# One 512-column product for two of 256 in an attention kernel's split score tiles, nine transposed loads instead of ten, and a new written-out order

## The chip, the cores and the metric

One Trainium2 chip, one of its cores. The metric is the device time of one execution in microseconds (us). The kernel before takes 271.66 us (median of three runs, 271.43 to 271.73).

## What is computed

The reference has two stages, cut here to what matters:

```python
# q, k, v: 4 x 5056 x 256, fp32
qn = q / (norm(q, axis=1) + 1e-6);  kn = k / (norm(k, axis=1) + 1e-6)   # norms down the 5056 rows
a  = softmax(kn.transpose(0, 2, 1) @ qn / tau)                          # 256 x 256 for each batch
x  = (v @ a).reshape(20224, 256)
logits = x @ phi                                                        # 32 slots
slots  = softmax(logits, axis=0).T @ x                                  # over all 20224 rows
out_s  = relu(slots @ w1[e]) @ w2[e]                                    # 8 experts, 4 slots each
out    = softmax(logits, axis=1) @ out_s                                # 20224 x 256
```

The softmax down the rows needs every row of v before the first expert can start, and every row of the output needs the experts. So all of q, k, v and the experts' weights are read before most of the 21 MB of output can be written.

## The kernel before, in words

Four batches follow each other. Each has ten pairs of q and k blocks (`u` = 0 to 39, 512 rows of each, 1 MB a load) and five v blocks (`p` = 0 to 19, 1 MB each).

- **Scores.** For each 128-row tile `j` of a block, TensorE adds k'q into a PSUM tile `S`, 256 x 256, kept as two channel halves `m` of 128 rows by 256 columns in one bank (`sums`, `score`). A tile with `j >= NS[u]` is multiplied in fp32 (`raw`). The other 117 tiles are split in two parts, high (cast by ScalarE in `cast`) and low (raw minus high, by GpSimd in `low`), both fp32r, and three products are added with k's parts as the weights: high x high, high x low, low x high, each of 256 columns.
- **Norms.** ScalarE squares a block (`square`), VectorE adds the squares into two PSUM banks `A` (`add`).
- **Per batch** (`att_*`): ScalarE copies both halves of `S` to SBUF (`att_evict`), VectorE scales them by the norms, ScalarE takes the softmax, and `a` is folded with phi into a small matrix `M`.
- **v blocks.** The logits need v transposed. For the blocks in `LT` the transposed copy `x` is loaded from HBM as well (`load_vt`, 1 MB). For the others TensorE turns the block in 16 transposes (`turn`), and four copies of 128 x 512 by ScalarE or VectorE bring it from PSUM (`turned`, `DVE_TURNED`). `logits` fills `L`, `gather` sums v by weight into `G`.
- **Experts.** 16 loads of 1 MB (`w1`, `w2`), products `H` and `O`. `O` for output half 0 needs the four loads w2_0_*, half 1 the four w2_1_*.
- **Output.** `out_mul` into `op`, copies by ScalarE and VectorE (`out_evict`), stores of 1 MB (`store`). Stores named oh hold one half of the channels and can start when half 0 is done; those named o need both halves.

All DMAs, loads and stores, are issued by SyncE (SP) in one queue. The order of the whole program is written by hand as a list of numbers, `ORDER`: each names an entry of the plan that `at(...)` collects, and the entries are issued in that order, so the list alone sets what stands before what on each engine. SBUF is 23 slots of 8 KB a partition; `SLOTS` says which tile takes which slot and `BANKS` which of PSUM's eight banks. A load waits until the readers of its slot's last tile are done, and every later DMA waits behind it.

Of the kernel before, what the change touches and what calls it, by code (L numbers as in the profile page):

```python
# [24 lines left out]
NT = [3 if u % (2 * UB) == 2 * UB - 1 else 4 for u in range(NU)]  # L25
NS = [0, 2, 2, 2, 2, 2, 2, 2, 2, 2, 3, 3, 3, 3, 3, 3, 3, 3, 3, 3, 3, 3, 3, 3, 3, 3, 3, 3, 3, 3, 4, 4, 4, 4, 4, 4, 4, 4, 4, 3]

LT = {4, 5, 6, 7, 8, 9, 10, 11, 12, 13}
# [1071 lines left out]
```

## Time and profile before

| | before |
|---|---|
| device time, median of 3 runs | 271.66 us (271.43 to 271.73) |
| profiled execution, span from first to last instruction | 269.6 us |
| device time of the profiled execution itself | not listed apart; the median less the span is 2.0 us |
| TensorE, VectorE, ScalarE, GpSimd busy | 91, 75, 77, 63% of the span |
| HBM read and written | 89.43 MB and 20.97 MB |
| mean rate of the DMA queue | 409 GB/s over the span |

The page cuts the span into 40 slices with a digit for the busy tenths of each engine, and lists the costliest groups of instructions, the chain of work that ended last and the DMA queues. The answers of the trace read one stretch more closely: a table of stretches (`windows`), the chain in order of time, and the timeline of one engine.

### The profile page before, as it was taken

Reading aid. Unit: us, or ns where it says so; the run is one execution under the profiler, and the core shown is the slowest. Engines: PE = TensorE matmul, PEld = TensorE weight load, DVE = VectorE, ACT = ScalarE, POOL = GpSimd, SP = SyncE. Lnnn points to the kernel's source line nnn. Section 1 sums busy time; section 2 is a strip of 40 time slices with the busy share of each in tenths; the row PEclk is TensorE's granted clock in tenths of the full one; section 3 lists DMA queues with packets and bytes.
Section 4 is the critical chain, followed back from the end, with each engine's and each line's share of the span. In section 5 each row is a group of like instructions: output and inputs, shape, how many; then the busy total and the mean of one; then the engine's idle time right before and its main releaser. Section 6 shows DMA issues by size and latency. Waiting matters only on the chain.

```text
span 269.6 us, 6368 instructions
## 1 busy us (share of the span) xinstructions
PE 244.9 (91%) x2490; PEld 205.4 (76%) x2490; DVE 201.0 (75%) x406; ACT 207.1 (77%) x331; POOL 169.6 (63%) x135
## 2 busy tenths in 40 slices
PE   6999999999999999999999999999999889989300
PEld 6799899999998987879879968985647677666200
DVE  1388688978799989889998788897785747795400
ACT  3999899999999999999999987586826536566200
POOL 1399989999999998989999999731206030000000
PEclk9999999999999999999999999999999999999555
DMA  7999999999999999999999999999999999999995
GB/s 272 428 424 419 417 419 420 423 418 416 424 414 419 422 417 422 423 414 416 421 421 418 420 427 413 420 420 422 413 423 422 412 418 395 420 424 422 424 425 227
DMA packets 15725, 110.80 MB, mean 411 GB/s; under 512 B 1872, under 2 KB 1872, under 8 KB 3024
## 3 DMA queue, kind: packets, MB, share of 16 engines
q1 hardware_dynamic: 15696, 110.40, 98.8%
q8 instruction: 19, 0.31, 0.5%
q14 instruction: 10, 0.08, 0.1%
HBM read 89.43 MB, written 20.97 MB: 409 GB/s over the span
## 4 chain that ended last, share of the span: by engine, by line
PE 78%; DMA 11%; DVE 2%; ACT 1%; issue 1%; SPq 0%; ACTq 0%
PE S L345 42%; PE L L512 7%; PE G L612 7%; PE T L492 6%; DMA w<-in_moe_w_dram 6%; PE op_None L845 4%; DMA out_dram<-o 3%; PE op L830 3%; DMA raw<-in_qk_dram 3%; PE H L762 2%; PE O L795 1%; PE Mp L445 1%; ACT o L862 1%; PE S L354 1%; PE nn L373 1%; PE aTp L433 1%
## 5 line engine op out<-in xcount | busy, mean ns | idle before, releaser
L292 POOL TENSOR_TENSOR hl<-raw,hl 128x512 fp32r<-128x512 f32 x117 | 146.5, 1291 | 14.3 <-ACT hl L288 14.3
L321 DVE TENSOR_TENSOR A<-sq,A 128x512 f32<-128x512 f32 (+1 forms) x144 | 94.5, 690 | 20.6 <-ACT sq L303 18.5
L345 PE MATMUL S<-hl 128*128 128x256 f32 x702 | 100.0, 292 | 0.0
L345 PEld LDWEIGHTS S<-hl 128*128 128x128 f32 x702 | 89.1, 190 | 3.5 <-issue 2.3
L303 ACT ACTIVATE sq<-raw 128x2048 f32<-128x2048 f32 (+2 forms) x40 | 71.6, 1806 | 0.2 <-DMA raw<-in_qk_dram 0.2
L288 ACT CAST hl<-raw 128x1024 fp32r<-128x1024 f32 (+1 forms) x69 | 61.0, 916 | 2.9 <-DMA raw<-in_qk_dram 1.4
L345 PE MATMUL S<-raw 128*128 128x256 f32 x156 | 38.3, 381 | 1.7 <-DMA raw<-in_qk_dram 1.7
L345 PEld LDWEIGHTS S<-raw 128*128 128x128 f32 x156 | 27.7, 190 | 5.2 <-DMA raw<-in_qk_dram 2.5
L492 PE MATMUL T<-ident,v 128*128 128x128 f32 x156 | 21.8, 274 | 0.5 <-DVE maxs L539 0.5
L710 POOL TENSOR_TENSOR nat<-nat,cm 128x1280 f32<-128x1280 f32 x4 | 9.4, 2352 | 19.0 <-DVE cm L707 19.0
L725 POOL TENSOR_TENSOR nat<-nat,cs 128x1280 f32<-128x1280 f32 x4 | 9.4, 2348 | 16.9 <-DVE cs L722 16.9
L862 ACT COPY o<-op_None 128x512 f32<-128x512 f32 x22 | 12.0, 592 | 10.2 <-PE op_None L845 9.0
L512 PE MATMUL L<-x,M 128*32 128x256 f32 (+1 forms) x320 | 19.3, 379 | 0.0
L492 PEld LDWEIGHTS T<-ident,v 128*128 128x128 f32 x156 | 17.8, 141 | 1.8 <-DVE maxs L539 0.7
L612 PE MATMUL G<-v,dn 128*32 128x256 f32 x312 | 18.7, 380 | 0.0
L830 PE MATMUL op<-cT,so 32*128 32x256 f32 x144 | 17.5, 417 | 0.7 <-ACT so L817 0.4
L862 DVE COPY oh<-op 128x256 f32<-128x256 f32 x36 | 12.9, 411 | 5.3 <-PE op L830 5.0
L862 DVE COPY o<-op_None 128x512 f32<-128x512 f32 x22 | 13.9, 680 | 2.7 <-PE op_None L845 2.6
L830 PEld LDWEIGHTS op<-cT,so 32*128 32x128 f32 x144 | 12.3, 183 | 4.3 <-ACT o L862 1.5
L612 PEld LDWEIGHTS G<-v,dn 128*32 128x32 f32 x312 | 10.7, 110 | 6.3 <-issue 0.5
L512 PEld LDWEIGHTS L<-x,M 128*32 128x32 f32 x320 | 10.3, 110 | 5.7 <-issue 0.7
L862 ACT COPY oh<-op 128x256 f32<-128x256 f32 x36 | 11.9, 384 | 2.7 <-PE op L830 2.7
(122 smaller groups left out, 279.8 us busy)
## 6 DMA issues: line engine op xcount, KB each, us to landing
raw<-in_qk_dram SPq DMA_DIRECT2D x38, 1024.0 KB, 13.6
v<-in_v_dram SPq DMA_DIRECT2D x16, 1024.0 KB, 13.8
w<-in_moe_w_dram SPq DMA_DIRECT2D x16, 1024.0 KB, 19.8
out_dram<-o SPq DMA_DIRECT2D x11, 1024.0 KB, 10.2
x<-in_vt_dram SPq DMA_DIRECT2D x10, 1024.0 KB, 13.5
out_dram<-oh SPq DMA_DIRECT2D x8, 1024.0 KB, 8.8
v<-in_v_dram SPq DMA_DIRECT2D x4, 896.0 KB, 13.8
raw<-in_qk_dram SPq DMA_DIRECT2D x2, 768.0 KB, 11.5
```

Of the source, the lines that this page charges most:

```text
L288: act.copy(parts(u, lo, hi)[:, :, 0::2, :], raws[u][:, lo:hi])
L292: pool.tensor_tensor(hl[:, :, 1::2, :], raws[u][:, lo:hi], hl[:, :, 0::2, :].bitcast(F32), op=ALU.subtract)
L303: act.activation(sqs[u][:, n : NT[u]], raws[u][:, n : NT[u]], AF.Square)
L321: dve.tensor_tensor(a[r], s[r, j], a[r], op=ALU.add)
L345: pe.matmul(S_[:, m], l, r, start=first, stop=False, skip_group_check=True)
L492: pe.transpose(tp[:, P * jj : P * jj + P], vtile(p, 4 * h + jj)[:, P * m : P * m + P], ident)
L512: pe.matmul(L[S * g : S * g + S, :n, :], M[:, m, :], x[:, :n, S * g : S * g + S], start=m == 0 and g not in void, stop=m == 1, skip_group_ ...
L612: pe.matmul(gp[S * g : S * g + S, :C], dn[:, x, j, :], vtile(p, j), start=x == 0 and j < G, stop=x == n - 1 and j >= G,)
L710: pool.tensor_tensor(nat[b], nat[b], st[b]["cm"].broadcast_to([P, 8 * PB, S]), op=ALU.subtract)
L830: pe.matmul(ops[b, p, hf, g], so[r, hf], cT[b][r, 8 * p : 8 * p + 8, :].rearrange("s j t -> s (j t)"), start=True, stop=True,)
L845: pe.matmul(ops[b, p, hf, g][:, h, :], cT[b][r, 4 * i : 4 * i + 4, :].rearrange("s j t -> s (j t)"), rhs[r], start=True, stop=True,)
L862: (dve.tensor_copy if g % 2 else act.copy)(dst, ops[b, p, hf, g])
```

## The change

Five things change.

1. **Joined products.** `S` takes two PSUM banks per batch, one for each channel half `m`. High x high and high x low have the same weights, so they become one product of 512 columns: columns 0 to 255 get high x high, columns 256 to 511 high x low. Low x high is added to columns 0 to 255. 702 products become 468.
2. **Sum of the halves.** `att_evict` is now a VectorE sum of the bank's two column halves (512 elements in, 256 out), in place of ScalarE's copy of 256.
3. **One more v block turned.** `LT` loses block 13: one 1 MB load less, 16 transposes and four copies more (two on VectorE, two on ScalarE).
4. **Memory.** Nine of the 23 slots stay slots of a pool, the other fourteen are slices of one SBUF tile, `arena`. All 1 MB inputs lie in one HBM tensor `one`, rows 8,704 bytes apart as before. The output tensor holds two stores side by side, so its rows lie 16 KB apart instead of 8 KB. Block q0 comes in four loads of 256 KB.
5. **Order, slots and banks** are new.

```diff
-LT = {4, 5, 6, 7, 8, 9, 10, 11, 12, 13}
+LT = {4, 5, 6, 7, 8, 9, 10, 11, 12}
...
+NT_SLOTS, NA_SLOTS = 9, 14
...
 ORDER = [
-    0, 1, 2, 3, 6, 8, 23, 24, 27, 25, 31, 33, 30, 28, 32, 26, 9, 7, 49, 51, 56, 57, 54, 35, 55, 59, 58, 34,
...
+    901, 10, 9, 0, 11, 1, 903, 34, 33, 12, 42, 17, 20, 35, 900, 902, 30, 21, 22, 899, 897, 898, 2, 15, 26,
...
+    arena = const.tile([P, NA_SLOTS, W], F32, name="arena")
+    def block(name):
+        if name not in blocks:
+            k = SLOTS[name]
+            if k < NT_SLOTS:
+                blocks[name] = large.tile([P, W], F32, tag=f"s{k}", name=name)
+            else:
+                blocks[name] = arena[:, k - NT_SLOTS]
+        return blocks[name]
+    def load(g):
+        n = sum(cols(x) for x in GROUPS[g])
+        src = (one, two)[len(GROUPS[g]) - 1][PLACE[g]]
+        sp.dma_start(run_of(GROUPS[g])[:, :n], src[:, :n])
+    def load_first(j):
+        x = slice(2 * C * j, 2 * C * j + 2 * C)
+        sp.dma_start(block("q0")[:, x], one[PLACE[0]][:, x])
...
-            st[b]["S"] = bank(f"S{b}").rearrange("p (m c) -> p m c", m=2)
+            st[b]["S"] = [bank(f"S{b}_{x}") for x in range(2)]
...
             if j >= NS[u]:
-                parts_ = [(raws[u][:, j, 1, cols], raws[u][:, j, 0, :])]
-            else:
-                k, x = split[u, j]
-                hl = hls[k][:, x]
-                parts_ = [(hl[:, w, cols], hl[:, y, :]) for w, y in ((2, 0), (2, 1), (3, 0))]
-            for l, r in parts_:
-                pe.matmul(S_[:, m], l, r, start=first, stop=False, skip_group_check=True)
-                first = False
+                mul(m, raw(u)[:, j, 1, cols], raw(u)[:, j, 0, :], 0, C)
+                continue
+            k, x = split[u, j]
+            hl = hls[k][:, x]
+            mul(m, hl[:, 2, cols], hl[:, 0:2, :].rearrange("p y c -> p (y c)"), 0, 2 * C)
+            mul(m, hl[:, 3, cols], hl[:, 0, :], 0, C)
...
     def att_evict(b, m):
-        act.copy(st[b]["ssb"][:, m], st[b]["S"][:, m])
+        both = st[b]["S"][m].rearrange("p (y c) -> p c y", y=2)
+        dve.tensor_reduce(mine(b, "ssb", [P, 2, C], "ssb")[:, m], both, axis=AX.X, op=ALU.add)
...
+    def store(g):
+        n = W // 2 if OUTS[g][0] in HALF else W * len(OUTS[g])
+        k, x = OPLACE[g]
+        sp.dma_start(oa[k][:, x * W : x * W + n], run_of(OUTS[g])[:, :n])
```

Each group in `GROUPS` and `OUTS` has one name, so every load and store stays one block of 1 MB or less.

**Where the order moves things.** TensorE late in batch 3's scores, before: the split tiles of block pairs (hl47, hl48, ...) stand between the turns of v blocks 14 and 19.

```order
L492 MATMUL T19_1_1_1909<-ident_72,v19_1670 128x128 x3
L492 MATMUL T19_1_1_1909<-ident_72,vh_78 128x128
L492 MATMUL T14_0_1_1914<-ident_72,v14_1637 128x128 x4
L345 MATMUL S3_1401<-hl47_1833 128x256 x6
L345 MATMUL S3_1401<-hl48_1863 128x256 x6
L345 MATMUL S3_1401<-hl41_1828 128x256 x6
```

The same place now (the v block that T13 reads is in the arena, which has one name):

```order
L546 MATMUL T14_0_1_1632<-ident_73,arena_72 128x128 x4
L546 MATMUL T13_1_0_1637<-ident_73,arena_72 128x128 x4
L408 MATMUL S3_0_1282<-hl47_1599 128x512
L408 MATMUL S3_0_1282<-hl47_1599 128x256
L408 MATMUL S3_1_1283<-hl47_1599 128x512
L408 MATMUL S3_1_1283<-hl47_1599 128x256
```

A split tile's six products of 256 columns are now four, two of 512 and two of 256, and turns of block 13 stand among them.

SP at the end of the loads, before: the last w1 load, the eight w2 loads and the first stores.

```order
L754 DMA w2_0_2_2705<-in_moe_w2_dram 128x2048
L754 DMA w2_1_2_2718<-in_moe_w2_dram 128x2048
L754 DMA w2_1_3_2720<-in_moe_w2_dram 128x2048
L754 DMA w2_1_1_2722<-in_moe_w2_dram 128x2048
L754 DMA w2_1_0_2846<-in_moe_w2_dram 128x2048
L869 DMA out_0_dram<-oh0_0_0_2841 128x2048
L869 DMA out_0_dram<-oh0_1_0_2869 128x2048
L869 DMA out_0_dram<-oh1_0_0_2895 128x2048
L869 DMA out_0_dram<-oh1_1_0_2921 128x2048
L872 DMA out_0_dram<-oh0_2_0_3020 128x1024
L866 DMA out_0_dram<-o2_0_3038 128x2048
```

And now:

```order
L264 DMA w2_0_2_2486<-in_one_dram 128x2048
L264 DMA w2_1_1_2524<-in_one_dram 128x2048
L264 DMA arena_72<-in_one_dram 128x2048
L264 DMA w2_1_0_2527<-in_one_dram 128x2048
L264 DMA arena_72<-in_one_dram 128x2048
L911 DMA out_0_dram<-oh0_2_0_2545 128x1024
L911 DMA out_0_dram<-oh1_1_0_2558 128x2048
L911 DMA out_0_dram<-oh0_1_0_2585 128x2048
L911 DMA out_0_dram<-arena_72 128x2048
L911 DMA out_0_dram<-oh1_0_0_2684 128x2048
L911 DMA out_0_dram<-oh0_2_1_2745 128x1024
```

Four w2 loads still stand between w2_0_2 and the first store, and 4.5 MB of half-0 stores before the first store of half 1; the first store is now one of 512 KB.

TensorE's first products, before, and then now (q_107 is block 1, q_139 block 3):

```order
L255 MATMUL wake_122<-ones 128x128 x8
L345 MATMUL S_139<-raw_131 128x256 x4
L345 MATMUL S_139<-raw_144 128x256 x4
L345 MATMUL S_139<-raw_131 128x256 x4
L345 MATMUL S_139<-hl_146 128x256 x6
```

```order
L324 MATMUL wake_130<-ones 128x128 x8
L408 MATMUL S_0_146<-q_139 128x256
L408 MATMUL S_1_147<-q_139 128x256
L408 MATMUL S_0_146<-q_107 128x256
L408 MATMUL S_1_147<-q_107 128x256
L408 MATMUL S_0_146<-hl_111 128x512
```

The first product read the first load; it now reads the second one (SP's queue begins with q1, q3 and a quarter of q0).

## Rows read from the trace of the kernel before

**Rows 1.** The page: span, DMA slices, packets and the DMA queue.
```profile
span 269.6 us, 6368 instructions
...
DMA  7999999999999999999999999999999999999995
...
q1 hardware_dynamic: 15696, 110.40, 98.8%
...
HBM read 89.43 MB, written 20.97 MB: 409 GB/s over the span
```

**Rows 2.** Table of stretches: length, busy of each engine, clock, DMA share, GB/s.
```profile
core 0: us, PE busy (x) PEld busy (x) DVE busy (x) ACT busy (x) POOL busy (x), PEclk, DMA share, GB/s
...
20.00:60.00 40.00, 40.00 (x273) 37.06 (x272) 32.74 (x51) 38.57 (x38) 38.77 (x33) 1.00 1.01 419
60.00:100.00 40.00, 40.00 (x345) 37.50 (x344) 34.93 (x66) 39.91 (x54) 40.00 (x34) 1.00 1.02 420
100.00:140.00 40.00, 40.00 (x448) 33.67 (x449) 37.29 (x75) 39.55 (x57) 37.28 (x31) 1.00 1.01 419
140.00:180.00 40.00, 39.51 (x423) 34.95 (x419) 34.63 (x69) 32.58 (x68) 33.44 (x25) 1.00 1.01 420
180.00:213.00 33.00, 32.22 (x504) 19.92 (x497) 24.08 (x61) 18.38 (x49) 8.35 (x4) 1.00 1.02 420
213.00:216.00 3.00, 3.00 (x36) 2.37 (x34) 2.75 (x9) 2.53 (x9) 0.00 (x0) 1.00 0.96 401
...
224.00:228.00 4.00, 3.66 (x47) 3.00 (x47) 3.33 (x9) 2.61 (x8) 0.00 (x0) 1.00 0.92 379
228.00:266.00 38.00, 22.38 (x198) 16.01 (x194) 19.20 (x40) 14.69 (x34) 0.00 (x0) 0.79 1.01 422
```

**Rows 3.** The chain in order of time: start us, us, what.
```profile
8.19 24.27 PE S L345 x146
...
76.99 0.44 PE T L492 x4
77.43 1.44 PE S L345 x12
...
80.75 0.81 PE Mp L445 x8
...
100.33 0.87 PE S L345 x4
...
197.64 5.31 PE H L762 x48
202.95 15.05 DMA w<-in_moe_w_dram
```

**Rows 4.** SP's timeline: start us, us, DMA issues.
```profile
213.83 4.74 SPq L869 DMA_DIRECT2D out_dram<-oh  x4
224.34 0.33 SPq L872 DMA_DIRECT2D out_dram<-oh  x1
226.30 0.33 SPq L866 DMA_DIRECT2D out_dram<-o  x1
...
254.34 1.24 SPq L866 DMA_DIRECT2D out_dram<-o  x1
```

**Rows 5.** DMA issues by line: KB each, median us from issue to landing.
```profile
raw<-in_qk_dram SPq DMA_DIRECT2D x38, 1024.0 KB, 13.6
```

**Rows 6.** The queue from 86.8 to 88.2 us, with 2 KB rows of the 256 KB load vh.
```profile
DMA packets 141, 0.60 MB, mean 429 GB/s; under 512 B 19, under 2 KB 19, under 8 KB 84
...
q1 hardware_dynamic: 141, 0.60, 106.6%
```

**Rows 7.** Groups by shape: busy us, mean ns of one, idle before.
```profile
L497 DVE COPY x<-T 128x512 f32<-128x512 f32 x20 | 13.2, 678 | 1.0 <-PE T L492 0.6 <-POOL nat L710 0.5
...
L497 ACT COPY x<-T 128x512 f32<-128x512 f32 x20 | 11.3, 586 | 1.4 <-PE T L492 1.2
...
L368 ACT COPY ssb<-S 128x256 f32<-128x256 f32 x8 | 2.9, 372 | 1.0 <-PE S L345 1.0
...
L378 DVE TENSOR_REDUCE rn<-nn 128x4 f32<-128x512 f32 x4 | 2.7, 676 | 0.7 <-PE nn L373 0.7
```

**Rows 8.** Timeline at the start and at the first output.
```profile
5.70 1.99 PE L345 MATMUL S<-raw 128*128 128x256 f32 x8 [1.23 <-DMA raw<-in_qk_dram]
8.16 1.05 ACT L288 CAST hl<-raw 128x1024 fp32r<-128x1024 f32 x1 [0.40 <-DMA raw<-in_qk_dram]
8.19 3.72 PE L345 MATMUL S<-raw 128*128 128x256 f32 x16 [0.49 <-DMA raw<-in_qk_dram]
...
211.49 6.11 PE L830 MATMUL op<-cT,so 32*128 32x256 f32 x64 [0.35 <-ACT so L817]
```

More of the change, by code (lines that the diff above doesn't have):

```diff
@@ L38, with cols, places @@
 WAKES = ((-8, 8),)
-ORDER = [
[60 rows of a table removed]
+NT_SLOTS, NA_SLOTS = 9, 14
+GROUPS = [
[9 rows of a table added]
+]
+OUTS = [
+    ("oh0_0_0",), ("oh0_0_1",), ("oh0_1_0",), ("oh0_1_1",), ("oh1_0_0",), ("oh1_0_1",), ("oh1_1_0",),
+    ("oh1_1_1",), ("oh0_2_0",), ("oh0_2_1",), ("o1_4",), ("o2_0",), ("o2_1",), ("o2_2",), ("o2_3",),
+    ("o2_4",), ("o3_0",), ("o3_1",), ("o3_2",), ("o3_3",), ("o3_4",),
+]
+ORDER = [
[61 rows of a table added]
 ]
 SLOTS = {
[26 rows of a table removed]
[25 rows of a table added]
 }
 BANKS = {
[36 rows of a table removed]
-}
[37 rows of a table added]
+}
+W = 8 * C
+def cols(name):
+    u = int(name[1:]) if name[0] in "qv" else 0
+    return 2 * C * NQ[u] if name[0] == "q" else W - C if name[0] == "v" and u % PB == PB - 1 else W
+def places(groups):
+    n, at = [0, 0], []
+    for g in groups:
+        at.append(n[len(g) - 1])
+        n[len(g) - 1] += 1
+    return at, n
+PLACE, NLOAD = places(GROUPS)
+x, (n, m) = places(OUTS)
+OPLACE = [(k, 0) if len(g) == 2 else (m + k // 2, k % 2) for g, k in zip(OUTS, x)]
+NOUT = m + (n + 1) // 2
+HALF = {f"oh{b}_2_{h}" for b in range(2) for h in range(2)}
 def run(plan):
@@ L180, in colnorm_attention_soft_moe @@
     tc: tile.TileContext,
-    qk: bass.AP,
-    v8: bass.AP,
-    vt8: bass.AP,
+    one: bass.AP,
+    two: bass.AP,
     vhalf: bass.AP,
     few: bass.AP,
-    w1: bass.AP,
-    w2: bass.AP,
     oa: bass.AP,
@@ L200, in colnorm_attention_soft_moe, with run_of @@
     ps = ctx.enter_context(tc.tile_pool(name="ps", bufs=1, space=PSUM, reuse_waits="tile"))
-    def slot(name, shape, dt=F32):
-        return large.tile(shape, dt, tag=f"s{SLOTS[name]}", name=name)
+    arena = const.tile([P, NA_SLOTS, W], F32, name="arena")
+    blocks = {}
+    def block(name):
[6 more added lines that the diff above has]
+        return blocks[name]
+    def run_of(names):
+        if len(names) == 1:
+            return block(names[0])
+        k = SLOTS[names[0]] - NT_SLOTS
+        assert SLOTS[names[1]] == k + 1 + NT_SLOTS
+        for x in names:
+            block(x)
+        return arena[:, k : k + 2].rearrange("p k w -> p (k w)")
+    def load(g):
[5 more added lines that the diff above has]
+        sp.dma_start(block("q0")[:, x], one[PLACE[0]][:, x])
     def short(name):
-        t = slot(name, [P, 2 * C, 4]).rearrange("p c x -> p (c x)")
-        return t[:, : 8 * PB * S].rearrange("p (j s) -> p j s", s=S)
+        return block(name)[:, : 8 * PB * S].rearrange("p (j s) -> p j s", s=S)
     def bank(name):
@@ L237, in colnorm_attention_soft_moe, with mine @@
     now = {}
+    def mine(b, key, shape, tag):
+        if key not in st[b]:
+            st[b][key] = bpool.tile(shape, F32, tag=tag, name=f"{key}{b}")
+        return st[b][key]
     def constants():
@@ L255, in wake, with raw, sq @@
             pe.matmul(w[:, :P], ones, ones, start=True, stop=True)
[L259 to L266 removed]
+    hls = {}
+    def raw(u):
+        return block(f"q{u}").rearrange("p (j x c) -> p j x c", x=2, c=C)
+    def sq(u):
+        return block(f"sq{u}").rearrange("p (j x c) -> p j x c", x=2, c=C)
     split = {}
@@ L325, in join, with sums, mul @@
         dve.tensor_tensor(a, st[b]["odd"], a, op=ALU.add)
-    def sums(b):
+    begun = set()
+    def sums(b, m):
         if "S" not in st[b]:
-            st[b]["S"] = bank(f"S{b}").rearrange("p (m c) -> p m c", m=2)
-            return st[b]["S"], True
-        return st[b]["S"], False
+            st[b]["S"] = [bank(f"S{b}_{x}") for x in range(2)]
+        first = (b, m) not in begun
+        begun.add((b, m))
+        return st[b]["S"][m], first
     def score(u, j):
         b, i = divmod(u, UB)
-        S_, first = sums(b)
+        def mul(m, l, r, lo, hi):
+            S_, first = sums(b, m)
+            pe.matmul(S_[:, lo:hi], l, r, start=first, stop=False, skip_group_check=True)
         for m in range(2):
@@ L477, in vtile @@
         b, q = divmod(p, PB)
-        return vh[:, b // 2] if q == PB - 1 and j == 7 else vs[p][:, j]
+        return vh[:, b // 2] if q == PB - 1 and j == 7 else block(f"v{p}").rearrange("p (j c) -> p j c", c=C)[:, j]
     def xt(p):
-        if p not in xs:
-            xs[p] = slot(f"x{p}", [P, 2, 8 * P])
-        return xs[p]
-    def load_vt(p):
-        b, q = divmod(p, PB)
-        sp.dma_start(xt(p), vt8[b, q][:, : 16 * P].rearrange("p (m t) -> p m t", m=2))
+        return block(f"x{p}").rearrange("p (m t) -> p m t", m=2)
     def turn(p, h, m):
@@ L772, in relu @@
         if r not in hss:
-            hss[r] = slot(f"hs{r}", [P, 2 * F])[:, :F]
+            hss[r] = block(f"hs{r}")[:, :F]
         act.activation(hss[r][:, x * UT : x * UT + UT], hps[r, x], AF.Relu, scale=rz[:, r : r + 1])
@@ L784, in back_h @@
         if r not in hTs:
-            hTs[r] = slot(f"hT{r}", [P, 2 * NF, P])[:, :NF]
+            hTs[r] = block(f"hT{r}").rearrange("p (f c) -> p f c", c=P)[:, :NF]
         (act.copy if x else dve.tensor_copy)(hTs[r][:, 4 * x : 4 * x + 4, :], htp[r, x])
@@ L888, in colnorm_attention_soft_moe @@
         b, i = divmod(u, UB)
-        if u == 0:
-            at(-3, load_qk, 0, 0, 4)
-        else:
-            at(-2.9 if u < 5 else u - 5 + 0.9, load_qk, u, 0, NT[u])
         for lo, hi in runs[u]:
             at(u - 1.0 + 0.1 * lo, cast, u, lo, hi)
-        late = u in SAME
-        at(u + 0.5 if late else u - 0.95, square, u)
+        at(u - 0.95, square, u)
         for lo, hi in runs[u] if u >= JOINED else [(j, j + 1) for j in range(NS[u])]:
             at(u - 0.5 + 0.1 * lo, low, u, lo, hi)
-        js = [2, 3] if i == 0 else [0, 1, 3, 2] if i == UB - 1 and b % 2 == 0 else list(range(NT[u]))
+        js = [2, 3] if i == 0 else [0, 1, 3, 2] if i == UB - 1 and b % 2 == 0 else list(range(NQ[u]))
         if i == 0 and b % 2:
@@ L902, in colnorm_attention_soft_moe @@
         for x, j in enumerate(js):
-            at(u + (0.55 if late else 0.4) + 0.1 * x, add, u, j)
+            at(u + 0.4 + 0.1 * x, add, u, j)
         if i == UB - 1:
@@ L906, in colnorm_attention_soft_moe @@
         halves = i == UB - 1 and b % 2 == 0
-        js = [j for j in range(NT[u]) if j >= NS[u] and not (halves and j == 3)] + list(range(NS[u]))
+        js = [j for j in range(NQ[u]) if j >= NS[u] and not (halves and j == 3)] + list(range(NS[u]))
         for x, j in enumerate(js):
@@ L918, in colnorm_attention_soft_moe @@
         k = when(p)
-        at(min(k - 7 if p < 5 else k - 4, 42), load_v, p)
-        if p in LT:
-            at(min(k - 6.9 if p < 5 else k - 3.9, 42.1), load_vt, p)
-        else:
+        if p not in LT:
             for h in range(2):
@@ L986, in colnorm_attention_soft_moe @@
     at(3.6, load_vh)
-    for e in range(8):
-        at(42.2 + 0.01 * e, load_w1, e)
-    for h in range(2):
-        for k in range(4):
-            at(T0 - 1 + 0.3 * k + h, load_w2, h, k)
+    for j in range(4):
+        at(-5, load_first, j)
+    for g in range(1, len(GROUPS)):
+        at(-5, load, g)
     for b in range(B):
@@ L1024, in colnorm_attention_soft_moe @@
                 at(t + 0.1, out_evict, b, p, None, g)
-            at(t + 0.2, store, b, p, None)
+            OAT[f"o{b}_{p}"] = t + 0.2
             t += 0.5
+    for g, names in enumerate(OUTS):
+        at(max(OAT[x] for x in names), store, g)
     run(plan)
@@ L1055 @@
     x = x.reshape(B, UB, 4, P, 2 * C).transpose(0, 1, 3, 2, 4)
-    add("qk", apart(x.reshape(B, UB, P, 8 * C)))
+    data = {f"q{u}": x.reshape(NU, P, 8 * C)[u] for u in range(NU)}
     x = np.zeros((B, PB * 8, P, C), np.float32)
@@ L1061 @@
     x = x.reshape(B, PB, 8, P, C)
-    add("v8", apart(x.transpose(0, 1, 3, 2, 4).reshape(B, PB, P, 8 * C)))
-    x = x.reshape(B, PB, 8 * P, 2, P).transpose(0, 1, 4, 3, 2)
-    add("vt8", apart(x.reshape(B, PB, P, 16 * P)))
+    y = x.reshape(B, PB, 8 * P, 2, P).transpose(0, 1, 4, 3, 2).reshape(NP, P, W)
+    x = x.transpose(0, 1, 3, 2, 4).reshape(NP, P, W)
+    for p in range(NP):
+        data[f"v{p}"], data[f"x{p}"] = x[p], y[p]
+    w1, w2 = (np.asarray(inputs[x]) for x in ("moe_w1", "moe_w2"))
+    x = w2.reshape(4, 2, P, 8, 2, P).transpose(4, 0, 2, 1, 3, 5).reshape(8, P, W)
+    for e in range(8):
+        data[f"w1_{e}"], data[f"w2_{e // 4}_{e % 4}"] = w1[e].reshape(P, W), x[e]
+    for k, name in enumerate(("one", "two")):
+        if not NLOAD[k]:
+            args.append(None)
+            continue
+        a = np.zeros((NLOAD[k], P, (k + 1) * W), np.float32)
+        for g, x in zip(GROUPS, PLACE):
+            if len(g) == k + 1:
+                a[x] = np.concatenate([data[y] for y in g], axis=1)
+        add(name, apart(a))
     add("vh", v[:, nf:].reshape(2, P, C).transpose(1, 0, 2))
```

138 lines of the change are left out of this document (48 added, 90 removed), and 252 rows, old and new, of tables (BANKS, GROUPS, ORDER, SLOTS).

## The prediction

> **What bounds the kernel now.** I read the page first, for what is full over the whole span; then the table of stretches, for where it is full; then the chain, SP's timeline and the DMA rows, for how far each other engine is from taking over.
>
> The DMA queue is the bound. Its packets took 98.8% of the span, 0.988 x 269.6 = 266.4 us [rows 1]. From 20 to 213 us its share is 1.01 to 1.02 at 419 or 420 GB/s, and again from 228 to 266 us (1.01 at 422) [rows 2]. There are two dips: 0.96 over 3 us and 0.92 over 4 us. Against 1.01 they leave 0.15 + 0.36 = 0.5 us of room [rows 2].
>
> The reader should also see that the chain of waits says something else. TensorE is busy in 40.00 of 40 us from 20 to 140 [rows 2], and the chain runs through its score products [rows 3]. But near the end that chain runs into a DMA wait of 15.05 us from 202.95 [rows 3]: had TensorE been faster up to there, this wait would have been longer. So a microsecond less on TensorE is worth nothing while the queue is full, and a microsecond less of bytes is worth a microsecond, on one condition: that each DMA is handed over in time. For the loads there is room: one takes 13.6 us from issue to landing [rows 5], of which 1.0486 MB at 419 GB/s needs 2.5, so some 11 us of it is waiting in the queue. For the first store there is none known: SP issued it at 213.83 [rows 4], and the first dip is at 213 to 216 [rows 2].
>
> The sum is made against the profiled execution, span 269.6; the median of the runs, 271.66, lies 2.06 above it, and I let that difference stand.
>
> **The change, part by part.**
>
> *Bytes.* One load of 1 MB goes: 1.0486 MB / 419 GB/s = **-2.50 us**. The output's bytes are the same. Block q0 comes in quarters, whose rows are 2 KB instead of 8 KB. The nearest row is the 256 KB load of vh, in a stretch of 1.4 us: 0.60 MB at share 106.6%, thus 1.066 / 429 against 1.01 / 419 elsewhere, 3% more queue time a byte [rows 2, 6]. About 0.26 of those 0.60 MB are such packets, so they cost some 3% x 0.60 / 0.26 = 7.5% more: 0.075 x 2.50 = **+0.19 us**. The ends are 0 and twice that. The 1 MB input tensors become one, with the same distance of rows, and I cost that at nothing, since each load moves the same packets. The sum for the queue is **-2.31 us**. The 0.5 us of the dips may be filled; I leave them (they are the low end).
>
> *TensorE, which is covered by the queue, unless it is late for the first store.* A split product of 256 columns takes 1.44 / 12 = 0.120 us from start to start, and one of 32 columns (Mp) still 0.81 / 8 = 0.101 [rows 3]. An instruction thus has a floor, and 0.120 is near it. In fp32, 256 columns take 0.87 / 4 = 0.217, and 128 columns (T) 0.44 / 4 = 0.110 [rows 3], at a granted clock of 1.00 [rows 2], the 2.4 GHz level: two cycles a column. H, with 512 columns and four products side by side, takes 5.31 / 12 = 0.44 a set [rows 3], so cost grows with columns up to 512. For fp32r I take one cycle a column: 512 columns in 0.217, the pair in 0.217 + 0.120 = 0.337 instead of 0.360. There are 117 tiles x 2 halves = 234 pairs, so 234 x 0.023 = **-5.4 us**. Ends: nothing, if 0.120 is the price of 256 columns and not a floor (512 then take 0.240); and 234 x 0.042 = -9.8, if the single product sinks to the 0.101.
>
> Against this stand the turns of block 13, 16 x 0.110 = **+1.8**, and the start: the first product stood at 5.70, on the first load, with 8 passes done before the second load's products at 8.19 [rows 8]; it now needs the second load, which puts 8 x 0.217 = **+1.7** behind it. Net -1.9 us: H starts at 195.7 instead of 197.64. From H to the first store took 213.83 - 197.64 = 16.2 us [rows 3, 4], in which TensorE went through H, O and the first output products [rows 8]. The first store is now 512 KB, so it needs half of the 2.34 us from 211.49 [rows 4, 8]: 1.2 less. It can go at 195.7 + 16.2 - 1.2 = 210.7. The reads end 2.3 us earlier, so it is wanted at 213.83 - 2.31 = 211.5. It makes that by **0.8 us**. The margin is used up at a pair of 0.340 us; at 0.350 the first store is as late as before.
>
> The Trainium skill, "TensorE: Matmul & The Clock Gate", § Back-to-back issue gap, gives 518 cycles for 512 columns and 262 for 256. By it the pair would be 325 ns, the saving 8.2 us and the margin 3.6; but its 109 ns for 256 columns is not the 0.120 of this trace [rows 3], and the trace's number stands in the sum.
>
> *VectorE and ScalarE.* Eight sums of 512 from PSUM take the time of the reduction of that shape, 8 x 0.676 = +5.4, and two copies of T13 2 x 0.678 = +1.4 [rows 7]. That is 6.8 us more for VectorE, which from 20 to 180 us was idle for 160 - 139.6 = 20.4 us [rows 2]. ScalarE gives up 8 x 0.372 and takes 2 x 0.586: -1.8 [rows 7]. What VectorE's idle time covers costs nothing; without that cover, each evict is later by 0.676 - 0.372 = 0.30 us, 8 x 0.30 = 2.4 in all. What waits there is `M`, hence the logits, hence v's slots and the loads queued behind them on SP, which have the 11 us above.
>
> *Order, slots, the arena.* A late release matters only beyond those 11 us. I cost the new order at nothing on that ground, and its upper end is in the second rival.
>
> **Sum:** 271.66 - 2.31 = 269.35, so **269.4 us**; by itself 268.8 (dips filled) to 269.9 (half a microsecond of new dips, as much as the old order has).
>
> **The rivals.**
>
> *Mid-stream gaps, 269.9 to 271.8, likeliest 270.6.* A slot comes free too late for its load, through the later `M`, the held v block of T13, or because the arena is one tile, so that a load into one slice waits for another's readers. It would cost up to the 2.4 us of the evicts if all were on the path, half of it as a middle. Against it: 11 us of lead [rows 5], and a share of 1.01 or more over 193 us [rows 2], so the old order had no such gap. For it: a new order has its own releases.
>
> *TensorE is late for the first store: 269.4 to 274.0, on the other side at the end.* One mechanism, at the joined product. If it takes 0.240 the pair saves nothing, TensorE is 3.5 us later at H, and the first store goes at 197.64 + 3.5 + 16.2 - 1.2 = 216.1. That is 4.6 after 211.5, in which the queue stands empty: 269.4 + 4.6 = 274.0. It decides from a pair of 0.340, and is slower than the kernel before from 0.350. For it: TensorE has no idle time [rows 2], and a row of fp32r at 512 columns is not in this trace. Against it: the floor seen at 32 columns, and the proportion seen in fp32 [rows 3].
>
> *Stores with rows 16 KB apart run slower: 271.8 to 274.8.* The 20.97 MB at 401 or at 379 GB/s, the lowest rates of a stretch, instead of 420 [rows 1, 2], take 52.3 or 55.3 us instead of 49.9: +2.4 or +5.4. Those two rates are better explained by stores handed over late, so this has little. The Trainium skill, "DMA: Bandwidth & Descriptors", § Latency and other measured facts, reports lower rates where rows lie a large power of two apart, 207 against 214 GB/s at 512 KiB; no run here shows it, and by that 3% of the stores' time the sum would be some 271.0, an estimate.
>
> That one load goes is plain from the list of loads; that it would not shorten a queue at 98.8% I give no chance of its own.
>
> **How the numbers follow.** A measurement of this kernel tells from no change what is over 0.2%, 0.54 us: faster is below 271.12, slower above 272.20. The forecast has 0.64, all faster. Mid-stream gaps 0.14: 0.10 faster, 0.03 same, 0.01 slower. TensorE late 0.16: 0.03, 0.06, 0.07. Slow stores 0.06: 0.01 same, 0.05 slower. Together 0.77, 0.10 and 0.13. The range goes from 268.7 (dips filled, quarters for almost nothing) to 271.6; above it stays most of the slow half of the second rival and the third, some 0.15.
>
> **What would show it.** Right: q1 with 109.35 MB and again 98 to 99% of a span of some 267.3; share 1.01 or more in every stretch from 20 us to the first store; a pair of S products in 0.337; H at about 195.7 and SP's first store at about 210.7, before the last load has landed. Wrong: a dip in share before 200 us (mid-stream gaps, and the load behind it names the slot); a first store after 211.5 with a dip behind the loads (TensorE late, and the pair tells why); a share of 1.01 at a lower rate from 228 us on (slow stores); or no product of 512 columns that is shorter than two of 256.

## The result and the profile after

The changed kernel takes **275.13 us** (median of 4 runs, 273.57 to 276.50) against 271.55 us (271.41 to 271.73): a ratio of **1.013, interval 1.009 to 1.017**. It is slower by 3.6 us; the prediction was 269.4 us, range 268.7 to 271.6. The profiled execution took 276.03 us, so its span of 274.3 lies near the upper end of the runs. The ratios below leave out executions over 1.5% above the kernel's fastest, and the profile of `again`, of 281.29 us, is such a one and is not read.

The page of the changed kernel, the rows that answer to [rows 1]:

```profile
span 274.3 us, 5939 instructions
...
DMA  7999999999998999999999999999999997999995
GB/s 276 417 421 418 424 422 420 410 424 422 412 418 337 375 362 361 424 422 419 418 412 421 415 384 403 424 423 421 417 421 418 394 415 326 415 416 421 409 405 244
...
q1 hardware_dynamic: 15984, 109.36, 97.5%
...
HBM read 88.38 MB, written 20.97 MB: 399 GB/s over the span
```

The load is gone (109.36 MB instead of 110.40), yet the queue's share fell only by 1.3 points, and 0.975 x 274.3 = 267.4 us of packet time is 1.0 us more than before, for 1% fewer bytes. The share digits hide what the rates show: four slices of 337 to 375 GB/s, one of 326.

The table of stretches of the kernel before (columns as in [rows 2]), cut where the changed kernel's rate falls:

```profile
84.00:92.00 8.00, 8.00 (x72) 7.89 (x69) 7.24 (x12) 8.00 (x10) 8.00 (x7) 1.00 1.02 420
92.00:110.00 18.00, 18.00 (x213) 15.41 (x212) 16.71 (x36) 17.91 (x30) 16.47 (x15) 1.00 1.01 420
...
200.00:220.00 20.00, 18.68 (x323) 13.18 (x319) 13.53 (x32) 10.50 (x26) 6.08 (x3) 1.00 1.01 417
220.00:232.00 12.00, 11.06 (x167) 8.80 (x158) 7.50 (x19) 6.58 (x19) 0.91 (x1) 1.00 0.99 408
232.00:266.00 34.00, 18.38 (x161) 12.70 (x160) 15.80 (x31) 11.60 (x25) 0.00 (x0) 0.76 1.01 422
```

The same table, changed kernel, with one stretch more, from 140 to 180:

```profile
84.00:92.00 8.00, 8.00 (x88) 6.22 (x87) 6.76 (x14) 7.82 (x11) 8.00 (x8) 1.00 0.82 310
92.00:110.00 18.00, 18.00 (x150) 14.66 (x152) 17.35 (x34) 17.61 (x26) 17.16 (x14) 1.00 1.00 374
...
140.00:180.00 40.00, 39.20 (x362) 32.47 (x362) 33.90 (x66) 29.32 (x51) 33.51 (x26) 1.00 1.01 410
...
200.00:220.00 20.00, 19.16 (x271) 12.89 (x272) 14.08 (x32) 9.99 (x22) 8.27 (x4) 1.00 0.99 410
220.00:232.00 12.00, 10.85 (x212) 8.02 (x210) 6.91 (x19) 5.30 (x17) 0.00 (x0) 1.00 0.89 366
232.00:266.00 34.00, 26.81 (x209) 19.42 (x206) 20.20 (x41) 15.47 (x35) 0.00 (x0) 0.80 1.00 412
```

The missing bytes, stretch by stretch, at 0.42 MB a us: 84 to 92, 8 x 110 / 420 = 2.1 us; 92 to 110, 18 x 46 / 420 = 2.0; 140 to 180, 40 x 10 / 420 = 1.0 ([rows 2] had 420); 200 to 220, 0.3; 220 to 232, 1.2; 232 to 266, 0.8. Together 7.4 us lost, less 2.5 for the load that is gone: +4.9, and the span grew by 4.7. Two thirds of the loss lie in the middle of the loads, most of that from 84 to 110 us.

Why the rate falls there: the DMA issues from 82 to 110 us, with the median time from issue to landing last, kernel before and then the changed one.

```profile
raw<-in_qk_dram SPq DMA_DIRECT2D x6, 1024.0 KB, 13.2
x<-in_vt_dram SPq DMA_DIRECT2D x3, 1024.0 KB, 13.6
```

```profile
arena<-in_one_dram SPq DMA_DIRECT2D x9, 1024.0 KB, 7.8
q<-in_one_dram SPq DMA_DIRECT2D x1, 1024.0 KB, 5.1
v<-in_one_dram SPq DMA_DIRECT2D x1, 1024.0 KB, 5.0
```

A load of 2.5 us used to stand in the queue for some 11 us; now it comes out 5 to 8 us after its issue. SP hands it over late, because its slot is not free. Slow transfers out of a full queue would come out later after their issue, not sooner.

On TensorE the first products are late and slow (timeline; [rows 8] has the place before), H starts at 202.39 instead of 197.57, and SP's first store goes at 217.89 instead of 213.83:

```profile
8.43 3.75 PE L408 MATMUL S<-q 128*128 128x256 f32 x8 [3.60 <-DMA q<-in_one_dram]
11.62 1.82 PE L408 MATMUL S<-hl 128*128 128x512 f32 x4
...
202.39 2.33 PE L810 MATMUL H<-arena,slT 128*32 128x512 f32 x17
```

```profile
217.89 4.23 SPq L911 DMA_DIRECT2D out_dram<-oh  x3
```

The queue was full until about then and not behind it:

```profile
213.00:217.00 4.00, 3.23 (x90) 2.75 (x86) 2.85 (x7) 0.59 (x2) 1.18 (x1) 1.00 1.02 418
217.00:220.00 3.00, 2.93 (x39) 2.39 (x32) 2.75 (x8) 2.50 (x8) 1.16 (x1) 1.00 0.86 355
```

### The profile page after: what moved, and what is told of

Same layout as the page of the kernel before. It is cut to its first block, busy times and chain, and to the rows that moved or that the text cites. A ratio compares the mean times of both kernels' runs of the same rounds, so it can differ in the third digit from the quotient of the medians.

```text
span 274.3 us, 5939 instructions
## 1 busy us (share of the span) xinstructions
PE 250.7 (91%) x2272; PEld 197.2 (72%) x2272; DVE 207.8 (76%) x416; ACT 206.9 (75%) x325; POOL 170.2 (62%) x135
## 3 DMA queue, kind: packets, MB, share of 16 engines
q1 hardware_dynamic: 15984, 109.36, 97.5%
## 4 chain that ended last, share of the span: by engine, by line
PE 84%; DMA 7%; issue 2%; ACT 2%; DVE 1%; DVEq 0%; SPq 0%; ACTq 0%
PE S L408 42%; PE T L546 7%; PE L L566 6%; PE G L666 6%; PE op L878 6%; PE op_None L893 5%; DMA arena<-in_one_dram 4%; PE O L843 3%; DMA q<-in_one_dram 3%; PE H L810 3%; PE Mp L511 1%; PE S L426 1%; PE hTp L828 1%; PE aTp L499 1%; PE wake L324 1%
## 5 line engine op out<-in xcount | busy, mean ns | idle before, releaser
L360 POOL TENSOR_TENSOR hl<-arena,hl 128x512 fp32r<-128x512 f32 x98 | 123.6, 1303 | 9.8 <-ACT hl L356 7.2
L408 PE MATMUL S<-hl 128*128 128x512 f32 x468 | 97.4, 353 | 0.0
L388 DVE TENSOR_TENSOR A<-sq,A 128x512 f32<-128x512 f32 (+1 forms) x68 | 45.6, 688 | 14.9 <-ACT A L369 12.7
L356 ACT CAST hl<-arena 128x1024 fp32r<-128x1024 f32 (+1 forms) x58 | 51.3, 911 | 2.0 <-PE S L408 1.9
L388 DVE TENSOR_TENSOR A<-arena,A 128x512 f32<-128x512 f32 (+1 forms) x76 | 51.0, 690 | 1.7 <-ACT arena L370 0.5
L370 ACT ACTIVATE arena<-arena 128x2048 f32<-128x2048 f32 (+1 forms) x17 | 30.7, 1812 | 0.7 <-ACT arena L370 0.3
L360 POOL TENSOR_TENSOR hl<-q,hl 128x512 fp32r<-128x512 f32 x19 | 24.1, 1289 | 7.5 <-ACT hl L356 7.5
L370 ACT ACTIVATE sq<-arena 128x2048 f32<-128x2048 f32 (+2 forms) x15 | 27.4, 1831 | 0.6 <-ACT rk L465 0.5
L408 PE MATMUL S<-arena 128*128 128x256 f32 x108 | 26.5, 380 | 0.0
L408 PEld LDWEIGHTS S<-arena 128*128 128x128 f32 x108 | 19.3, 189 | 2.8 <-issue 0.3
L878 PE MATMUL op<-cT,so 32*128 32x256 f32 x144 | 17.2, 423 | 1.4 <-ACT so L865 0.8
L878 PEld LDWEIGHTS op<-cT,so 32*128 32x128 f32 x144 | 11.6, 183 | 5.4 <-ACT arena L906 1.4
L893 PE MATMUL op_None<-so,cT 32*128 32x256 f32 x96 | 11.6, 470 | 0.2
## 6 DMA issues: line engine op xcount, KB each, us to landing
arena<-in_one_dram SPq DMA_DIRECT2D x59, 1024.0 KB, 11.6
```

The source lines that it names most:

```text
L356: act.copy(parts(u, lo, hi)[:, :, 0::2, :], raw(u)[:, lo:hi])
L360: pool.tensor_tensor(hl[:, :, 1::2, :], raw(u)[:, lo:hi], hl[:, :, 0::2, :].bitcast(F32), op=ALU.subtract)
L370: act.activation(sq(u)[:, n : NQ[u]], raw(u)[:, n : NQ[u]], AF.Square)
L388: dve.tensor_tensor(a[r], s[r, j], a[r], op=ALU.add)
L408: pe.matmul(S_[:, lo:hi], l, r, start=first, stop=False, skip_group_check=True)
L878: pe.matmul(ops[b, p, hf, g], so[r, hf], cT[b][r, 8 * p : 8 * p + 8, :].rearrange("s j t -> s (j t)"), start=True, stop=True,)
```

## The experiments

Three theories. **T**: TensorE is late for the first store. **G**: slots come free late in the middle, and the queue runs nearly dry. **P**: the stores with rows 16 KB apart are slower. The ratio is to the kernel before, with its interval; the us are that ratio of 271.5, as a difference.

| kernel | ratio | interval | us |
|---|---|---|---|
| changed kernel | 1.0131 | 1.0088 to 1.0173 | +3.6 |
| again (changed kernel) | 1.0115 | 1.0080 to 1.0151 | +3.1 |
| start | 1.0095 | 1.0069 to 1.0121 | +2.6 |
| wake | 1.0102 | 1.0077 to 1.0128 | +2.8 |
| start_fill | 1.0098 | 1.0080 to 1.0116 | +2.7 |
| split3 | 1.0172 | 1.0159 to 1.0185 | +4.7 |
| noturn13 | 1.0104 | 1.0080 to 1.0127 | +2.8 |
| nolow | 1.0015 | 0.9990 to 1.0041 | +0.4 |
| relief | 1.0125 | 1.0104 to 1.0147 | +3.4 |
| relief_start | 1.0147 | 1.0120 to 1.0175 | +4.0 |
| noadd | 1.0130 | 1.0061 to 1.0199 | +3.5 |
| nosq | 1.0211 | 1.0183 to 1.0240 | +5.7 |
| nosq_nolow | 0.9988 | 0.9953 to 1.0023 | -0.3 |
| noarena | 1.0145 | 1.0078 to 1.0211 | +3.9 |
| pitch8 | 1.0117 | 1.0085 to 1.0150 | +3.2 |
| b_nolow (kernel before) | 0.9997 | 0.9985 to 1.0008 | -0.1 |
| b_noload13 (kernel before) | 0.9962 | 0.9940 to 0.9984 | -1.0 |
| b_both (kernel before) | 0.9911 | 0.9898 to 0.9923 | -2.4 |
| b_wake (kernel before) | 1.0042 | 1.0028 to 1.0057 | +1.1 |

**Is the queue the bound, and is a load worth 2.5 us?** Four edits of the kernel before:

```diff
 b_nolow
-for w, y in ((2, 0), (2, 1), (3, 0))
+for w, y in ((2, 0), (2, 1))
 b_noload13
     def load_vt(p):
+        if p == 13:
+            return
...
-x = xs[p][:, m]
+x = xs[14 if p == 13 else p][:, m]
 b_both: the two together
 b_wake
-at(T0 - 0.3, wake, k, 8 + x)
+at(T0 - 0.3, wake, k + 7 * x, 8 + x)
```

> The kernel before without the low x high products of the split tiles (234 of 256 columns, 28 us of TensorE); all loads stay. If the queue is the bound: 270.5 to 271.5 us, the dips filled at best. Theory T with TensorE alone as the limit: the first store comes with the last load, also 270.5 to 271. If the other engines hold the work as tightly as TensorE, H moves by less than 3 us.

> The kernel before without the load of block 13's transposed copy: the logits of block 13 read block 14's copy instead, so one load of 1 MB is left out and no work is added on any engine. By the prediction's first term (the queue is the bound): 2.5 us less, 269 us. Theory T (compute sets the first store, and the span is the first store plus some 55.5 us): the first store stays at 213.8 us, the reads end 2.5 us sooner, and the time stays at 271 to 271.5 us with a dip ahead of the first store.

> The kernel before without that load and without the low x high products. The queue then has 2.5 us less to move and TensorE is early: if the queue is the bound once compute is early, 268 to 269 us. If other engines (ScalarE, VectorE, GpSimd) hold the first store too: 270 to 271 us.

> The kernel before with 7 more warm-up products just ahead of H (14 passes at 0.125 us: 1.75 us of TensorE that nothing covers); nothing else changes. If the span is the first store plus some 55.8 us whatever the queue does: the first store at 215.6 us, time 273.0 to 273.5. If the stores' queue takes up the lateness (a full queue from the first store on is all that counts, and reads still fill it to 214.9): 272.2 to 272.8. If TensorE had slack there: 271.5.

28 us less on TensorE change nothing (-0.1 us, and H moves only to 197.33): the queue bounds the kernel before, as the prediction said. With the load gone as well, the time falls by 2.4 us, the prediction's byte term (2.50) to a tenth. The page of b_both and its first store on SP:

```profile
span 267.8 us, 5898 instructions
...
q1 hardware_dynamic: 15552, 109.36, 98.5%
```

```profile
211.87 5.15 SPq L871 DMA_DIRECT2D out_dram<-oh  x4
```

The first store came 1.96 us earlier than in [rows 4], with the loads. Without that load alone it stayed at 213.83, and only 1.0 us was gained: TensorE held it. In b_wake, 1.6 us of lateness at H (199.20 for 197.57) moved the first store by as much, to 215.47, and cost 1.1 us: the price of a microsecond there is some 0.7. The first store of b_noload13, then H and the first store of b_wake:

```profile
213.83 4.74 SPq L871 DMA_DIRECT2D out_dram<-oh  x4
```

```profile
199.20 7.07 PE L762 MATMUL H<-w,slT 128*32 128x512 f32 x64
```

```profile
215.47 4.74 SPq L869 DMA_DIRECT2D out_dram<-oh  x4
```

**TensorE in the changed kernel.**

```diff
 start: run() issues the entries in this order
-score(3, 3), score(1, 2), ..., score(1, 3)
+score(1, 2), score(1, 3), score(3, 3), ...
 wake
-for _ in range(k):
+for _ in range(k + 16 * (n == 0)):
 start_fill: start, and wake(8, 7) in a spare bank ahead of score(1, 1)
 split3
-mul(m, hl[:, 2, cols], hl[:, 0:2, :].rearrange("p y c -> p (y c)"), 0, 2 * C)
+mul(m, hl[:, 2, cols], hl[:, 0, :], 0, C)
+mul(m, hl[:, 2, cols], hl[:, 1, :], C, 2 * C)
 noturn13: turn(13, ...) and turned(13, ...) return; logits(13) reads x14
 nolow
-mul(m, hl[:, 3, cols], hl[:, 0, :], 0, C)
```

> The changed kernel itself, for its spread and a second trace. All theories: between 273.5 and 276.5 us. Theory G (a slot released late by GpSimd, then slow packets): a trace whose time is lower has a smaller dip near 88 us and fewer packets over 0.6 us behind it, with the same first store less that dip. Theory T (TensorE is late for the first store): H and the first store move with the time, dip or not.

> TensorE's products of block 1, which the first load brings, go ahead of those of block 3, so TensorE starts near 5.6 us and not at 8.43, without the pause in which its clock falls. Theory T: the start gives back some 3.5 us on TensorE (1.7 of products at an earlier time, the rest from products at 0.426 us instead of 0.216), H starts near 199, the first store near 214.5, and the time falls to 271 to 273 us. Theory G, if the dip near 88 us comes of the late start: the dip goes and the time falls to 271 to 272.5; if it comes of the order: the dip stays at 2 us or more, and the time falls by less than 1 us. Theory P (the 16 KB output rows are slow): no change, 275.

> 16 more warm-up products ahead of the first score product, so TensorE's clock doesn't fall before 8.4 us; the first product still waits for the second load. Theory T: products from 8.4 to 13.9 us at 0.216 instead of 0.426, 2 to 2.7 us saved, H near 199.9, time 272 to 273.5 us. Theory G with a dip from the order: at most 0.5 us less. Theory P: no change.

> The start of TensorE on block 1 again, and 8 warm-up products between those products and the first split tile, where TensorE waited for GpSimd and its products then ran at a granted clock of 0.52. If TensorE's start is worth its time at the first store: H near 199.5 us, first store near 215, time 272.3 to 273.5 us and at least 0.7 us below the start alone. If the other engines hold H as tightly: the start alone's 273.6 to 274.7. No theory gives the 269.4 of the prediction, since the slots from 84 to 110 us stay late.

> The joined product undone: three products of 256 columns with the low part still in the second column half, and everything else as in the changed kernel. If the price goes by columns (0.234 us for 512, 0.117 for 256): TensorE 234 x 0.003 = 0.7 us later, time as the changed kernel's within 1 us, 274.5 to 276. If the join saves what the prediction reckoned (0.023 us a pair): 5.4 us later at H, time 278 to 280 us.

> The changed kernel without the turns of block 13 (16 transposes and their four copies are left out; its logits read block 14's copy). Theory T: H and the first store 1.8 us earlier, time 272 to 273.5 us. If what holds the changed kernel lies ahead of block 13's turns (before 175 us) or in the queue alone: less than 0.7 us gained, 274 to 275.

> Leaves out the low x high products of all split tiles (234 products of 256 columns, 234 x 0.117 = 27 us of TensorE), everything else as in the changed kernel. Theory T alone: the first store follows the last load, and the time falls to the queue's own 269 to 270 us. Theory G alone: GpSimd's work is unchanged, so the dip near 88 us stays and the time is 272 to 274. Theory P: 274 to 275, with a lower rate behind 228 us.

The start is worth at most some 1 us, not the 2 to 4 that T gave it, and it is not told apart from nothing: start, wake and start_fill lie 0.3 to 1.0 us below the two rows of the changed kernel, and the intervals overlap. H moved from 202.39 to 200.81, 200.90 and 200.65, but a profile of the changed kernel without its arena (noarena, below), with the start as it was, has H at 200.73 as well. There the same first products were done by 13.10 us instead of 13.96, and TensorE was busy for 40.00 us from 140 to 180 instead of 39.20: 0.86 + 0.80 is the whole of the 1.66 us. So H differs between two programs of the same list and work by as much as these edits seemed to gain. Nor did the first store follow H: 216.33 in start, but 218.06 in wake and 217.44 in start_fill, 17.2 and 16.8 us after H instead of 15.5; in these two the granted clock from 200 to 220 us was 0.91 and 0.92 instead of 1.00. The dip near 88 us stayed in all three (338, 335 and 374 GB/s).

```profile
217.44 4.23 SPq L917 DMA_DIRECT2D out_dram<-oh  x3
```

Undoing the join cost 1.1 us, with intervals that just overlap. TensorE's own times agree: from the first product of a split tile to the first one behind the tile, the mean over 117 tiles is 0.766 us in the changed kernel and 0.783 in split3, 1.9 us in all, and H came at 204.18. The join helps, by a third of what was reckoned. Block 13's turns were worth under 1 us, within the intervals. In noturn13's table one sees what the pause at the start does, from 8 to 16 us, after 3.8 us in which TensorE had nothing to do:

```profile
8.00:12.00 4.00, 3.57 (x9) 2.89 (x10) 0.00 (x0) 3.99 (x5) 2.99 (x3) 0.50 1.02 415
12.00:16.00 4.00, 4.00 (x16) 3.38 (x15) 1.17 (x2) 4.00 (x5) 4.00 (x4) 0.69 1.05 429
```

The granted clock is 0.50, the 1.2 GHz level. In wake, without the pause, the same eight passes took 1.99 us and not 3.75. Without the low x high products the changed kernel falls by 3 us, but stays 2.8 us above b_both, which has the same bytes and the same products left out. T is thus about half of the story, and not cleanly parted from the rest: H in nolow (198.10) is still 2.6 us behind that of b_both (195.46). In nolow the dip from 84 to 92 has gone, that from 92 to 110 has not:

```profile
84.00:92.00 8.00, 7.41 (x73) 4.76 (x72) 7.09 (x15) 8.00 (x12) 8.00 (x8) 1.00 1.02 414
92.00:110.00 18.00, 16.19 (x145) 11.09 (x143) 16.75 (x34) 18.00 (x26) 17.59 (x15) 1.00 0.99 384
```

**Whose work frees the slots late?** SP's waits from 60 to 132 us (us in total, times, longest), kernel before and changed kernel:

```profile
SPq L266 <- PE S L345: 19.5, 5, 5.3
SPq L468 <- DVE A L321: 10.4, 3, 4.0
...
SPq L266 <- POOL hl L292: 3.0, 5, 1.6
```

```profile
SPq L264 <- POOL hl L360: 25.3, 10, 5.2
SPq L264 <- DVE A L388: 10.4, 4, 4.5
SPq L264 <- PE S L408: 7.9, 3, 4.2
```

All rows of the two answers together are 61 us before and 63 after, so the sum of SP's waits doesn't tell a full queue from one that runs dry; the time from issue to landing does. TensorE freed the slots for 35 of those 61 us; of the 63, GpSimd is named for 25. So GpSimd, VectorE and ScalarE were relieved in turn:

```diff
 relief (relief_start: with start as well)
+WHOLE = {(3, 0), (4, 1), (7, 0), (7, 1), (12, 0)}
     def low(u, lo, hi):
+        if (u, lo) in WHOLE:
+            return
...
-            if j >= NS[u]:
+            if j >= NS[u] or (u, j) in WHOLE:
 noadd: add(u, j) returns for u in (4, 5, 6, 12, 13, 14); nosq: square(u) too
 nosq_nolow: nosq and nolow together
 noarena
-            if k < NT_SLOTS:
+            if k >= 0:
```

> The changed kernel with five early tiles of scores multiplied in fp32 instead of split: GpSimd computes no low part for them (5 x 1.29 = 6.5 us less), TensorE takes 0.87 instead of 0.70 us for each (0.9 us more). Theory G (slots come free late because GpSimd is behind, so the queue runs nearly dry from 85 to 110 us): the dip near 88 us and the packets over 0.6 us behind it mostly go, loads there take 10 us or more from issue to landing again, and the time falls to 272.5 to 274 us, where the late first store (217 us) still holds it. Theory T alone: nothing gained in the middle, H 0.9 us later, time 275 to 276 us.

> The same five fp32 tiles, and TensorE's products of block 1 ahead of those of block 3. Theories T and G together: no dip in the middle, first store near 215 us, time 270.5 to 272.5 us, and at least 1 us below either edit alone. Theory T alone: as with the start alone, 273.6 to 275 us. Theory G alone: as with the five tiles alone.

> The changed kernel without VectorE's adds of the squares for blocks 4, 5, 6, 12, 13 and 14 (24 adds of 0.69 us, 16 us of VectorE before 95 us are left out; the norms lack these blocks). If VectorE, with the sums of the score halves on it, releases the late slots from 84 to 110 us: the dip there goes, the rate of 92 to 110 us is 415 GB/s or more, and the time falls by 2 us or more, to 272 to 273. If ScalarE or the order of the list sets them: rate and time as in the changed kernel, 274 to 276.

> The same blocks without their squares on ScalarE too (6 x 1.9 = 11 us of ScalarE, and 16 us of VectorE; the norms lack these blocks). If ScalarE's work (it is busy 62.8 of 64 us from 20 to 84) sets the late slots: no dip from 84 to 110, loads there take over 10 us from issue to landing, and the time falls to 271.5 to 273, held by TensorE. If the order of the list alone does: the dip stays.

> Those squares and adds and the low x high products left out together. If the changed kernel's loss is lateness of its engines and nothing else (a full queue needs 2.3 us less than before): 269 to 270 us. If something in the transfers themselves costs more (rows 16 KB apart, quarters, one tensor for all inputs), or the slots are late by their order: 271 us or more.

> The fourteen slices of the arena are slots of the pool again, one tile for each block; the list, the slots and all the work stay. If loads wait for readers of other slices: the waits of 84 to 110 us go and 2 us or more with them, 271.5 to 273. If not: the changed kernel's time, 274 to 276.

G, as it was put, fell: 6.5 us less on GpSimd gained nothing, and SP waited for it just as long, 25.2 us:

```profile
SPq L267 <- POOL hl L365: 25.2, 10, 5.2
```

The dips stayed too (332 and 376 GB/s), and with the start as well (relief_start) nothing was gained, where both theories together gave 270.5 to 272.5 us. So the amount of work on the engine that is named is not at fault; that it is itself fed late is likely but was not tested. 16 us less on VectorE gained nothing measurable either (interval 1.006 to 1.020), and the dips stayed (346 and 377). The one tile for fourteen slots is not their cause: in noarena's profile, of a run of 273.56 us, they are as in the changed kernel. Only the loss from 140 to 180 us is not there, nor is it in pitch8's profile, which has the arena (419 GB/s), so that loss is of the one execution profiled:

```profile
84.00:92.00 8.00, 8.00 (x86) 6.17 (x86) 7.21 (x15) 7.83 (x10) 8.00 (x7) 1.00 0.88 337
92.00:110.00 18.00, 18.00 (x158) 14.44 (x160) 17.08 (x33) 17.60 (x27) 17.02 (x15) 1.00 0.99 379
140.00:180.00 40.00, 40.00 (x378) 33.25 (x368) 34.45 (x69) 30.24 (x56) 32.81 (x25) 1.00 1.01 419
```

nosq came out slower, which no theory gave; in its profile TensorE's granted clock was 0.83 from 200 to 220 us, its first store came 18.4 us after H (201.71) instead of 15.5, and the dip of 84 to 110 was there (317 and 375 GB/s). Why its runs are slower stays open.

```profile
200.00:220.00 20.00, 19.16 (x240) 10.62 (x241) 11.67 (x25) 8.03 (x16) 6.80 (x4) 0.83 0.89 369
```

```profile
220.07 4.23 SPq L915 DMA_DIRECT2D out_dram<-oh  x3
```

nolow alone had removed the first dip. With TensorE, ScalarE and VectorE all early, in nosq_nolow, the second is half as deep as in the changed kernel:

```profile
84.00:92.00 8.00, 7.68 (x71) 4.52 (x69) 7.39 (x16) 8.00 (x13) 8.00 (x8) 1.00 1.02 421
92.00:110.00 18.00, 16.34 (x147) 11.70 (x148) 16.80 (x31) 18.00 (x25) 17.83 (x15) 1.00 0.99 399
```

The nine runs behind its ratio go from 269.6 us (three of them, nearly what b_both takes) to 273.2, median 271.1. So the transfers themselves don't forbid 269.6; but most of its runs lie above the 269 to 270 that lateness alone was to give, and its interval overlaps nolow's.

**The stores.** Each store goes to a tensor of its own rows again:

```diff
 pitch8
-sp.dma_start(oa[k][:, x * W : x * W + n], ...)
+sp.dma_start(oa[2 * k + x][:, :n], ...)
```

> The output's rows 8 KB apart again, as in the kernel before, everything else as in the changed kernel. Theory P (rows 16 KB apart make stores slower): 2 us or more less, 272 to 273. Theories T and G: the changed kernel's time, 274 to 276.

No difference that these runs can tell: P falls, at least at the 2 us it asked for. The changed kernel's own rows agree: with stores 16 KB apart, start and noarena moved 419 and 418 GB/s from 232 to 266 us, the kernel before 422.

## Why the prediction was wrong

- **What bounds the kernel before, and the price of a load: right.** The queue (b_nolow), and 2.4 us measured for 2.5 reckoned, 2.31 with the quarters (b_both). The condition that the prediction set, each DMA handed over in time, is what the change broke.
- **"I cost the new order at nothing": the step that failed, and by the table of stretches the larger part.** The ground was 11 us of lead in [rows 5], and that lead belonged to the old program. In the new one a load from 82 to 110 us lands 5 to 8 us after its issue, and 84 to 110 us alone cost 4.1 us (3.3 in noarena's profile). The rival of gaps in the middle named the mechanism, but its price, at most 2.4 us from the evicts, came from one edit and not from the list. With the low x high products left out on both sides, the rest of the change costs 2.8 us (nolow against b_both). The cause of the late slots stays open. It is not the arena and not GpSimd's amount of work. The dip of 84 to 92 us went with TensorE's work (nolow), that of 92 to 110 only in part. Nor is it the amount of VectorE's work: noadd took 16 us off, and the dips stayed. Whether the list or the new slots set them was not tested, since no kernel between the two was built.
- **The pair of products at 0.337 us: mis-sized.** In the changed kernel's chain two pairs stand as follows:

```profile
86.48 0.70 PE S L408 x4
```

  That is 0.35 a pair; from start to start, 0.234 for 512 columns and 0.117 for 256. The prediction took 0.120 as the floor of an instruction, because 32 columns took 0.101; it was the price of 256 columns. The saving is 234 x 0.009 = 2 us and not 5.4; split3's tiles gave 1.9. The prediction's own threshold stood at 0.340, with the first store as late as before at 0.350, so its second rival came nearest: it priced a first store at 216.1 with 274.0 us.

  The Trainium skill, "TensorE: Matmul & The Clock Gate", § Back-to-back issue gap, gives 518 and 262 cycles, nearly a ratio of two, as here; the trace's durations are 7 to 8% longer. Its ratio was the better guide than the floor that the prediction drew from the 32 columns.
- **The start, +1.7 us: too small.** Eight passes from 8.43 us took 3.75 us and the next four products 1.82, against 1.99 for eight in [rows 8]: in the pause that the later first load makes, TensorE's clock falls, and the products to 13.96 us lose about 2 us more (1.5 in noarena's profile, to 13.10). The prediction moved the work and not the clock. 3.3 us from the pair and 2 from the start are most of the 6.7 by which H missed the 195.7; 0.8 more is TensorE's wait between 140 and 180 us.
- **The first store "with a margin of 0.8 us": wrong by 7.2** (217.89 for 210.7). It can't be added to the dips. The reads, held up in the middle, ended only about 217 us (share 1.02 from 213 to 217), so compute and loads arrived together; that each had waited for the other is argued, not shown. Behind it the stores lost 2 us more (220 to 266 us).
- **VectorE and ScalarE at nothing: not refuted.** noadd gained nothing. **T13:** its turns cost under 1 us of time, within the intervals.
- **The quarters of q0, +0.19 us: right by luck.** [rows 6] has 84 - 19 = 65 packets of 2 KB, 0.13 MB and not 0.26, so the step from the stretch to the packet doesn't hold. By the packets' own times in the kernel before, 0.0844 us for 2 KB and 0.315 for 8 KB, a byte costs 7% more, close to the 7.5% taken.

## What to carry to other kernels

Lead in a queue is a property of the whole program, its order and its slots, so it must be read again from the new order, load by load: what frees each slot, and when, not only what the old order had to spare. Where a queue at 99% and an engine at 40.00 of 40 us meet at one event, removing from the one pays only as much as the other is early there; b_noload13 and b_both, 1.0 and 2.4 us for one and the same load, show both cases. When SP's waits name an engine, relieve it before believing it: what fed that engine may be the limit. And a mark in one profile, such as H, shows an edit's effect only if it stays where it is without the edit; here it lay 1.7 us apart in two programs of the same list.
